# Gate weights loaded first, two weight splits moved into the attention, late rows transposed one group later

## The chip, the cores and the metric

One core of one Trainium2 chip runs the whole program. The metric is the device time of one execution in microseconds (us), the median over several runs. The engines are TensorE (PE, its weight loads PEld), VectorE (DVE), ScalarE (ACT), GpSimd (POOL) and SyncE (SP), which here only issues transfers.

## What is computed

The reference chains three stages over 4 batches of 576 tokens.

```python
# attention: 4 x 8 heads, 576 positions, 64 columns a head
scores = q @ k.T / sqrt(64) + min(-(cum_i - cum_j), 0)     # cum = cumsum(max(s, 0)); causal
x = softmax(scores) @ v                                    # -> x: 2304 tokens x 512
# one expert of 8 for each token, the one with the largest logit
logits = x @ w_gate                                        # w_gate: 512 x 8
x[t] = p_e * (relu(x[t] @ w1[e]) @ w2[e])                  # 512 -> 1024 -> 512
# gated unit on normalised rows
xn = x / rms(x) * rms_g
out = (silu(xn @ w_gate2) * (xn @ w_val)) @ w_out          # 512 -> 1536 -> 512
```

## The kernel before

**The attention** (`attention`, L573) works on 16 pairs of heads, `p` = 0 to 15. For each pair TensorE makes scores (`s_mm`, L269 to L284), VectorE adds the bias and takes the row extreme (L255), ScalarE takes exponentials (`s_exp`, L295), TensorE transposes the probabilities in seven groups (`t_mm`, L314), ScalarE copies them out of PSUM (L347), TensorE multiplies by `v` (`pv_mm`, L360 and L364), ScalarE copies the result (L370, L372), and TensorE turns it back to token rows (`o_mm`, L388). That last product has as its moving operand the tile `tg`: 128 columns of the identity, which turn the rows, and 16 columns of `w_gate`, which give the gate's logits in the same instruction.

The order of the work is written by hand. `attention` fills a list `plan` with (time, function) entries; a pair's step stands at 10 `p` plus an offset from the table `POS`, and single steps have times of their own. The entries are sorted by time and called in that order. What they emit for TensorE, VectorE, ScalarE and SP stays in that order on each engine; GpSimd's order is chosen by the scheduler. The times are only ranks: one unit of the plan is a little over a microsecond on the chip. Ahead of the plan stand the loads of pairs 0 and 1 (query, key, bias, and last `load_v` for both).

**The gate weights.** `gate_consts` (L122), planned at 14.0, makes `tg`: GpSimd clears the gate columns (L125), VectorE copies the identity (L126), SP issues two transfers of `w_gate` (L128), each 64 partitions x 4 x 8 numbers, told to come after the cumulated sums are stored. Planned just ahead of them, at 12.6 to 12.8, are three fills (`prefill`, L155) of 771 KB each, which preset rows of the scratch tensor `xs`.

**The weights of an expert** come as eight raw pieces of 512 KB in two halves for each of four units. `feed` (L647) issues the transfer of the next piece into one of four staging buffers, `split` (L658) makes a piece into a rounded part, by a cast on ScalarE (L666), and a remainder, by a subtraction on GpSimd (L667), and then may call `feed` once more. For the first expert, `feed` runs for two pieces at 60.0 and `split` at the six times of `PIECES` (L568), of which the first four fetch another piece. The unit that the last two pieces fill lies in a slot that held inputs of the attention's last pair.

**Routing and early rows.** When a batch is done, `route` (L412) finds each token's expert and its place (VectorE, L434 to L477), and GpSimd scatters the rows into `xs`, a region for each expert, by indirect transfers (L482). The last batch's steps are spread over the first expert by the counts in `RANK` (L977): so many steps behind each group. The first 256 rows of the first expert ("early") are loaded once the third batch is scattered: `EARLY_AT` has the load (152.2, L691), the scaling by the gate's probability (164.0, `gate`, L736) and the transposes (170.2, 170.3).

**The first expert** (`moe`, L877) fetches its last two pieces, runs eight groups of the first product (`gemm1`, L783), with a split behind groups 0 and 1, then four groups of the second (`gemm2`, L803). Its next 128 rows ("late") need the last batch's scatter: `load_late` (L705) is issued in the middle of `gemm1`, then the second expert's rows and its first four pieces. Behind group 0 of `gemm2` stands the scaling of the late rows, behind group 1 their transposes (`turn_tile`, L761), the first split of the second expert's weights behind those, then groups 2 and 3 and the row-wise product of the late rows (`rows_gemm1`, L835, L841). `moe` is emitted as a list of its own behind the attention's; in the trace its first two fetches stand earlier on SP's queue, between the attention's loads.

```python
    feed(k, 2)                                  # moe: the first expert's last two pieces
    for f in range(8):
        gemm1(k, 0, f, NA)
        ...
        if f < 2:
            split(k, 1, False)
    ...
    gemm2(k, 0, 0, NA)
    gate(k, k.xl, ((0, 128),))
    gemm2(k, 0, 1, NA)
    turn_tile(k, k.xl[:, 0, :], *xb)
    split(k)
    gemm2(k, 0, 2, NA)
```

Of the kernel before, what the change touches and what calls it, by code (L numbers as in the profile page):

```python
# [15 lines left out]
B, H, S, D = 4, 8, 576, 64  # L16
# [6 lines left out]
NA = 256  # L23
# [98 lines left out]
def gate_consts(k):  # L122
    nc = k.nc
    k.tg = k.apool.tile([128, H // 2, 144], F32, name="tg")
    nc.gpsimd.memset(k.tg[:, :, 128:144], 0.0)  # L125
    nc.vector.tensor_copy(k.tg[:, :, 0:128], k.ident.unsqueeze(1).broadcast_to((128, H // 2, 128)))  # L126
    for h, r in enumerate((slice(0, 64), slice(64, 128))):
        i = nc.sync.dma_start(out=k.tg[r, :, 128 + 8 * h:136 + 8 * h],  # L128
                              in_=k.w_gate.rearrange("d (a b) e -> d a b e", b=2)[:, :, h, :])
        after(k, i.ins, [k.cumdone])  # L130


def cumulate(k):
# [81 lines left out]
def attn_load(k, p):  # L215
    nc = k.nc
    st = k.st[p] = Ctx()
    st.q, st.k, st.cb, st.cm, st.bd = k.inp[p % 3]
    st.s = {}
    nc.sync.dma_start(out=st.q, in_=k.q[p])  # L220
    nc.sync.dma_start(out=st.k, in_=k.k[p])
# [179 lines left out]
def after(k, ins, earlier):  # L401
    for x in earlier:
        k.tc.add_manual_dep(ins, x.name, SYNC, reason="rows of one tensor")
# [161 lines left out]
)  # L565
ROUTE = (34.1, 0.2)
FR = 2
PIECES = (80.0, 81.5, 90.0, 91.5, 159.0, 166.0)  # L568
EARLY_AT = (152.2, 164.0, 170.2, 170.3)
FILL = (12.6, 12.7, 12.8, 22.6, 22.7, 22.8, 32.5, 32.6)  # L570

# [1 line left out]
def attention(k):  # L573
    k.st, k.todo = {}, []
    with ExitStack() as es:
        k.apool = es.enter_context(k.tc.tile_pool(name="attn", bufs=1))
        cum = cumulate(k)
        next(cum)
        masks(k)
        attn_statics(k)  # L580
        next(cum)
        attn_load(k, 1)
        for _ in cum:
            pass
        load_bias(k, 1)
        load_v(k, 0)
        load_v(k, 1)
        plan = []

        def add(at, fn, *a):  # L590
            plan.append((at, len(plan), fn, a))

        def step(j):
            next(j, None)

        k.order = [(0, u, q) for u in range(4) for q in (0, 2)]
        k.staged, k.xq, k.who = [], {}, {}

        for p in range(NP):
            for tag, fn in (("S", s_mm), ("X", s_exp), ("T", t_mm), ("V", pv_mm), ("W", pv_out), ("O", o_mm)):  # L600
                for i, at in enumerate(POS[tag]):
                    add(10 * p + at, fn, k, p, i)
            add(10 * p + POS["N"][0], s_norm, k, p)
            for h, at in enumerate(POS["Q"]):
                add(max(10 * p + at, 0.5), q_diag, k, p, h)
            for fn, at in zip((attn_load, load_bias, load_v), POS["Z"]):
                if p > 1:
                    add(10 * p + at, fn, k, p)
            j = route(k, p // 4)
            if p == NP - 1:  # L610
                k.last = j
            elif p % 4 == 3:
                for n in range(RSTEPS):
                    add(10 * p + ROUTE[0] + ROUTE[1] * n, step, j)
        add(60.0, feed, k, FR)
        for n, at in enumerate(PIECES):
            add(at, split, k, 1, n + FR < len(PIECES))
        add(EARLY_AT[0], load_early, k)
        add(EARLY_AT[1], lambda k: gate(k, k.x[0], EARLY), k)
        add(EARLY_AT[2], lambda k: x_transpose(k, 0, (0, 1), EARLY), k)  # L620
        add(EARLY_AT[3], lambda k: x_transpose(k, 0, (2, 3), EARLY), k)
        add(13.0, rank_consts, k)
        add(14.0, gate_consts, k)
        for n in range(FILLS):
            add(FILL[n], prefill, k, n)
        for at, n, fn, a in sorted(plan, key=lambda x: x[:2]):
            fn(*a)
# [19 lines left out]
def feed(k, n=1):  # L647
    for _ in range(n):
        if k.order:
            s, u, q = k.order.pop(0)  # L650
            raw = staging(k, [2, 512], F32)
            src = (k.w1, k.w2)[u // 2]
            src = src[0, u % 2] if s == 0 else src[bass.ds(who(k, s), 1), u % 2].rearrange("e p q n -> (e p) q n")
            k.nc.sync.dma_start(out=raw, in_=src[:, q:q + 2, :])
            k.staged.append((s, u, q, raw))


def split(k, n=1, refill=True):  # L658
    nc = k.nc
    for _ in range(n):  # L660
        if k.staged:
            s, u, q, raw = k.staged.pop(0)
            if q == 0:
                new_unit(k, s, u)
            w = k.wt[s, u][:, q:q + 2]
            nc.scalar.copy(w[:, :, 0, :], raw)  # L666
            nc.gpsimd.tensor_tensor(w[:, :, 1, :], raw, w[:, :, 0, :].bitcast(F32), op=ALU.subtract)  # L667
            if refill:
                feed(k)
# [66 lines left out]
def gate(k, x, tiles):  # L736
    for t, m in tiles:
        k.nc.scalar.activation(x[0:m, t, 0:DM], x[0:m, t, 0:DM], AF.Copy, scale=x[0:m, t, DM + 1:DM + 2])
# [138 lines left out]
def moe(k, close):  # L877
    k.y, k.sq = {}, {}

    def rank(n):  # L880
        for _ in range(n):
            next(k.last, None)

    feed(k, 2)
    k.order = [(s, u, q) for s in range(1, E) for u in range(4) for q in (0, 2)]
    row = ids(k, k.x[0], EARLY)
    keep_ids(k, row, 0)
    rank(RANK[0])
    for f in range(8):
        gemm1(k, 0, f, NA)  # L890
        rank(RANK[f + 1])
        if f == 3:
            load_late(k)
        if f < 2:
            split(k, 1, False)
    load_x(k, 1)
    feed(k, STG)
    first = tiles_of(CAP[0])
    gemm2(k, 0, 0, NA)
    rank(1)  # L900
    gate(k, k.xl, ((0, 128),))
    gemm2(k, 0, 1, NA)
    rank(1)
    xb = [k.rpool.tile([128, 4, CM], F32R, name=f"xb{n}", tag=f"xt{n}", bufs=1)[:, :, 0:128] for n in range(2)]
    turn_tile(k, k.xl[:, 0, :], *xb)
    row = ids(k, k.xl, ((0, 128),))
    keep_ids(k, row, column(k, 1))
    split(k)
    gemm2(k, 0, 2, NA)
    gate(k, k.x[1], first)  # L910
    split(k)
    gemm2(k, 0, 3, NA)
    split(k)
    k.hr = y_tile(k, "hr")[:, 0:1024]
    rows_gemm1(k, xb, 0)
    split(k)
    rows_gemm1(k, xb, 1)
    hb = [k.mpool.tile([128, 8, CM], F32R, name=f"hb{n}", tag=f"h{n}")[:, :, 0:128] for n in range(2)]
    turn_tile(k, k.hr[:, 0:512], *[t[:, 0:4] for t in hb])
    x_transpose(k, 1, (0, 1), first)  # L920
    turn_tile(k, k.hr[:, 512:1024], *[t[:, 4:8] for t in hb])
    x_transpose(k, 1, (2, 3), first)
    split(k)
    y = finish(k, 0, NA)
    row = ids(k, k.x[1], first)
    yr = k.hr.rearrange("p (a n) -> p a n", a=2)
    k.yr = yr[:, 0, :]
    rows_gemm2(k, hb)
    keep(k, y, NA, 0)
    keep_ids(k, row, column(k, 2))  # L930
    split(k)
    head = iter(())
    for s in range(1, E):
        last = s == E - 1
        n = CAP[s - 1]
        if last:
            close()
            glu_first(k)
            next(head)
        else:  # L940
            load_x(k, s + 1)
        for f in range(8):
            gemm1(k, s, f, n)
            if s == 1 and f == 0:
                y = yr[:, 1, :].rearrange("p (c n) -> p c n", c=4)
                turn_rows(k, k.yr, y)
            if s > 1 and f == 1:
                y = finish(k, s - 1, CAP[s - 2])
            if f == 5:
                keep(k, y, CAP[s - 2] if s > 1 else LATE, column(k, s))  # L950
                if not last:
                    gate(k, k.x[s + 1], tiles_of(CAP[s]))
            if f % 2 or (s == 1 and f < 4):
                split(k)
            next(head, None)
        for c in range(4):
            gemm2(k, s, c, n)
            if not last:
                if c in (1, 2):
                    x_transpose(k, s + 1, (2 * c - 2, 2 * c - 1), tiles_of(CAP[s]))  # L960
                if c == 1:
                    row = ids(k, k.x[s + 1], tiles_of(CAP[s]))
                if c == 3:
                    keep_ids(k, row, column(k, s + 2))
            split(k)
            if s == E - 2 and c == 0:
                head = glu_head(k)
            next(head, None)
    assert not k.staged and not k.order

    def tail():
        keep(k, finish(k, E - 1, CAP[-1]), CAP[-1], column(k, E))

    k.tail = tail
# [764 lines left out]
```

## Time and profile before

| | us |
|---|---|
| median of 3 runs | 881.94 (880.71 to 884.03) |
| the profiled execution | 880.62 |
| its span, first to last instruction | 878.6 |
| granted TensorE clock, mean over the span | 0.987 |
| TensorE busy | 844.7 |

The trace is of one execution, whose own time is 880.62 us; the span is what its instructions cover. Rows of a timeline have the start in us, the duration in us, the engine, the line of the kernel, the operation, the output and its inputs by the program's names, and a count where neighbours are merged; a bracket has the time for which the engine was idle before it and what released it. A count xN with one duration is the stretch from the first start to the last end.

### The profile page before, as it was taken

The numbers are of one execution on the slowest core, as the hardware profiler recorded it, in microseconds if no ns is written. First come the engines' busy times: TensorE is split into PE (matmuls) and PEld (weight loads), VectorE is DVE, ScalarE is ACT, GpSimd is POOL, SyncE is SP. The second block draws the span as 40 slices with busy tenths as digits, with TensorE's granted clock in tenths as the row PEclk, the third lists the DMA queues.
The fourth block names the chain that finished last, engine by engine and source line by source line (L and its number), as shares of the span: only waits on it lengthen the run. The fifth ranks groups of instructions, "written<-read, shape, count | busy, mean of one in ns | idle before, by whom it ended". The sixth has DMA issues, their size and how long they took to land.

```text
span 878.6 us, 15491 instructions
## 1 busy us (share of the span) xinstructions
PE 844.7 (96%) x5522; PEld 754.1 (86%) x5522; DVE 513.7 (58%) x1241; ACT 455.4 (52%) x1069; POOL 366.4 (42%) x318
## 2 busy tenths in 40 slices
PE   6699999999899999999999999999999999999994
PEld 4477777769799999999999999999999988888883
DVE  5356666657433355335799998988898878400000
ACT  4688998883665565566553443333333244433310
POOL 3000422034476666767331332544444360466641
PEclk9899999999899999999999999999999999999997
DMA  6997887221765565557562433332222487520001
GB/s 210 291 308 237 263 254 214 82 79 56 222 198 185 183 206 191 171 192 208 184 220 100 141 109 102 114 106 92 102 103 101 138 323 316 194 95 37 36 37 40
DMA packets 60506, 141.45 MB, mean 161 GB/s; under 512 B 6992, under 2 KB 25451, under 8 KB 60419
## 3 DMA queue, kind: packets, MB, share of 16 engines
q1 hardware_dynamic: 57459, 130.83, 46.1%
q0 software_dynamic: 2912, 9.46, 2.9%
q8 instruction: 45, 0.74, 0.4%
q14 instruction: 42, 0.34, 0.1%
q10 hardware_dynamic: 48, 0.07, 0.0%
HBM read 105.42 MB, written 34.92 MB: 160 GB/s over the span
## 4 chain that ended last, share of the span: by engine, by line
PE 47%; DVE 3%; ACT 1%; issue 0%; POOL 0%; POOLq 0%; DVEq 0%; ACTq 0%
PE gg L1165 29%; PE go L1481 17%; PE g L803 1%; DVE raw L1094 0%; DVE ws L1142 0%; DVE gx1a L1409 0%; DVE raw L1097 0%; DVE h L787 0%; DVE raw L1093 0%; DVE sq L828 0%; DVE tmp L1187 0%; DVE tmp L1185 0%; ACT raw L1095 0%; ACT ws L1137 0%; DVE y L831 0%
## 5 line engine op out<-in xcount | busy, mean ns | idle before, releaser
L667 POOL TENSOR_TENSOR u<-raw,u 128x1024 fp32r<-128x1024 f32 x64 | 154.9, 2434 | 84.0 <-ACT u L666 83.8
L803 PE MATMUL g<-h,u 128*128 128x256 f32 (+7 forms) x768 | 107.8, 299 | 0.6 <-DVE h L787 0.3
L803 PEld LDWEIGHTS g<-h,u 128*128 128x128 f32 x768 | 103.4, 192 | 1.7 <-DVE h L787 0.8
L783 PE MATMUL g<-xt,u 128*128 128x256 f32 (+7 forms) x768 | 104.3, 295 | 0.0
L783 PEld LDWEIGHTS g<-xt,u 128*128 128x128 f32 x768 | 101.4, 188 | 0.8
L255 DVE CUSTOM_DVE_ANT_0 sc<-s,in 128x128 f32<-128x128 f32 (+3 forms) x128 | 57.8, 489 | 32.7 <-ACT vp L372 19.2
L295 ACT ACTIVATE p<-sc,nm 128x128 f32<-128x128 f32 (+3 forms) x128 | 71.0, 574 | 7.2 <-DVE nm L255 7.2
L1203 POOL TENSOR_TENSOR hs<-tmp,hs 128x384 f32<-128x384 f32 x27 | 30.3, 1123 | 106.0 <-ACT hs L1201 106.0
L666 ACT CAST u<-raw 128x1024 fp32r<-128x1024 f32 x64 | 67.1, 1049 | 4.2 <-DMA raw<-in_w 4.2
L1165 PE MATMUL gg<-gx2a,ws 128*128 128x384 f32 x360 | 67.4, 335 | 0.6 <-DVE tmp L1187 0.6
L1165 PE MATMUL gg<-gx0a,ws 128*128 128x384 f32 x360 | 67.7, 336 | 0.0
L1165 PE MATMUL gg<-gx1a,ws 128*128 128x384 f32 x360 | 67.1, 335 | 0.0
L1486 DVE COPY raw<-go 128x256 f32<-128x256 f32 x1 | 0.4, 425 | 109.3 <-ACT raw L1485 109.3
L811 DVE TENSOR_TENSOR sq<-sq,sn 128x256 f32<-128x256 f32 (+6 forms) x21 | 14.4, 688 | 84.1 <-ACT sn L810 84.1
L1165 PEld LDWEIGHTS gg<-gx2a,ws 128*128 128x128 f32 x360 | 62.7, 188 | 0.9 <-DVE tmp L1187 0.9
L1165 PEld LDWEIGHTS gg<-gx0a,ws 128*128 128x128 f32 x360 | 63.1, 188 | 0.0
L1165 PEld LDWEIGHTS gg<-gx1a,ws 128*128 128x128 f32 x360 | 62.7, 188 | 0.0
L347 ACT COPY pt<-t 128x512 f32<-128x512 f32 (+3 forms) x160 | 56.0, 448 | 10.3 <-PE t L314 9.1
L314 PE MATMUL t<-ident,p 128*128 128x128 f32 x400 | 51.8, 275 | 0.0
L1095 ACT ACTIVATE raw<-raw 128x512 f32<-128x512 f32 x36 | 24.5, 682 | 51.1 <-DVE raw L1094 32.9
L269 PE MATMUL s<-in 64*128 64x128 f32 (+3 forms) x256 | 49.5, 495 | 0.0
L360 PE MATMUL pvy<-pt,vp 128*64 128x512 f32 (+4 forms) x320 | 46.9, 428 | 1.1 <-ACT pt L347 1.1
(307 smaller groups left out, 1714.6 us busy)
## 6 DMA issues: line engine op xcount, KB each, us to landing
raw<-in_w SPq DMA_DIRECT2D x64, 512.0 KB, 4.7
hd<-hs SPq DMA_DIRECT2D x72, 192.0 KB, 1.9
in<-cumd SPq DMA_DIRECT2D x30, 256.0 KB
xs<-zrow SPq DMA_DIRECT2D x8, 771.0 KB, 10.6
raw<-in_wg SPq DMA_DIRECT2D x12, 512.0 KB, 4.1
raw<-in_wv SPq DMA_DIRECT2D x12, 512.0 KB
raw<-in_wo SPq DMA_DIRECT2D x12, 512.0 KB, 7.6
vp<-in_v SPq DMA_DIRECT2D x16, 320.0 KB, 5.2
```

Source lines behind the costliest of these rows:

```text
L255: k.nc.vector.tensor_tensor_reduce(out=out, in0=ps, in1=bias, scale=-0.125, scalar=3e38, op0=ALU.add, op1=ALU.min, accum_out=accum)
L269: nc.tensor.matmul(ps[h], st.q[r, 128 * i:128 * i + 128], st.k[r, 0:w], start=True, stop=False)
L295: k.nc.scalar.activation(out, st.s[i, h][:, 0:w], AF.Exp, bias=st.nm[:, n:n + 1], scale=-1.0, accum_out=acc)
L314: nc.tensor.transpose(ps[:, off:off + 128], src[:, 128 * j:128 * j + 128], k.ident)
L347: nc.scalar.copy(b, a)
L360: nc.tensor.matmul(st.y[r, a - 64:512], st.v[:, h, j, :], k.pt[:, h, o:o + S - a], start=j == 0, stop=j == 4)
L666: nc.scalar.copy(w[:, :, 0, :], raw)
L667: nc.gpsimd.tensor_tensor(w[:, :, 1, :], raw, w[:, :, 0, :].bitcast(F32), op=ALU.subtract)
L783: nc.tensor.matmul(ps[:, 0:n], w[:, f % 4, a, 128 * kc:128 * kc + 128], x[b][:, kc, 0:n], start=kc == 0 and i == 0, stop=kc == 3 and i == 2)
L803: nc.tensor.matmul(ps[:, 0:n], w[:, f % 4, a, 128 * c:128 * c + 128], k.h[b][:, f, 0:n], start=f == 0 and i == 0, stop=f == 7 and i == 2)
L1165: k.nc.tensor.matmul(k.ps[u, bank], w[:, a, 128 * c:128 * c + 128], x[:, b, GT * c:GT * c + GT], start=first and c == 0 and n == 0, stop=c ...
L1481: k.nc.tensor.matmul(acc[g][t], c[:, a, cols], w[:, b, :], start=f == 0 and i == 0, stop=f == NF - 1 and i == 2)
```

## The change

Three edits. `gate_consts` is planned at 0.7 instead of 14.0, without VectorE's copy of the identity, which becomes `gate_ident` and stays at 14.0. `PIECES` has eight times instead of six, and the number that decides whether a split fetches another piece follows its length, so that six of them do; the two fetches and the two splits in the first expert go. In the first expert the scaling of the late rows moves behind group 1 of the second product, and group 2 is put ahead of their transposes.

```diff
@@ gate_consts
     nc.gpsimd.memset(k.tg[:, :, 128:144], 0.0)
-    nc.vector.tensor_copy(k.tg[:, :, 0:128], k.ident.unsqueeze(1).broadcast_to((128, H // 2, 128)))
     for h, r in enumerate((slice(0, 64), slice(64, 128))):
...
+def gate_ident(k):
+    k.nc.vector.tensor_copy(k.tg[:, :, 0:128], k.ident.unsqueeze(1).broadcast_to((128, H // 2, 128)))
@@
-PIECES = (80.0, 81.5, 90.0, 91.5, 159.0, 166.0)
+PIECES = (80.0, 81.5, 90.0, 91.5, 159.0, 161.7, 164.4, 167.1)
@@ attention
-        add(14.0, gate_consts, k)
+        add(0.7, gate_consts, k)
+        add(14.0, gate_ident, k)
@@ moe
-    feed(k, 2)
...
-        if f < 2:
-            split(k, 1, False)
...
     gemm2(k, 0, 0, NA)
     rank(1)
-    gate(k, k.xl, ((0, 128),))
     gemm2(k, 0, 1, NA)
     rank(1)
+    gate(k, k.xl, ((0, 128),))
+    gemm2(k, 0, 2, NA)
...
     turn_tile(k, k.xl[:, 0, :], *xb)
     row = ids(k, k.xl, ((0, 128),))
     keep_ids(k, row, column(k, 1))
     split(k)
-    gemm2(k, 0, 2, NA)
     gate(k, k.x[1], first)
     split(k)
     gemm2(k, 0, 3, NA)
```

## Rows read from the trace of the kernel before

**Rows 1.** The page, part 1: busy us, share of the span, instructions.

```profile
PE 844.7 (96%) x5522; PEld 754.1 (86%) x5522; DVE 513.7 (58%) x1241; ACT 455.4 (52%) x1069; POOL 366.4 (42%) x318
```

**Rows 2.** Timeline of TensorE: the wait for `tg`, and the same step later.

```profile
39.49 1.30 PE L388 MATMUL tl<-tg,vp 128*128 128x144 f32 x4 [6.87 <-DMA tg<-in_w_gate]
...
43.33 1.14 PE L360 MATMUL pvy<-pt,vp 128*64 128x512 f32 x4
...
162.10 0.93 PE L314 MATMUL t<-ident,p 128*128 128x128 f32 x7
...
164.78 1.08 PE L360 MATMUL pvy<-pt,vp 128*64 128x512 f32 x4
```

**Rows 3.** Timeline of SP's queue, 12 to 36 us: issues of transfers.

```profile
14.85 0.43 SPq L220 DMA_DIRECT2D in<-in_q  x1
...
15.80 1.31 SPq L228 DMA_DIRECT2D in<-cumd  x2
...
29.67 2.69 SPq L128 DMA_DIRECT2D tg<-in_w_gate  x2
```

**Rows 4.** Timeline of VectorE: the first use of pair 2's bias.

```profile
27.43 0.29 DVE L255 CUSTOM_DVE_ANT_0 sc<-s,in 128x128 f32<-128x128 f32 x1 [1.43 <-DMA in<-cumd]
```

**Rows 5.** Timeline of ScalarE at the end of the attention.

```profile
190.91 2.36 ACT L347 COPY pt<-t 128x512 f32<-128x512 f32 x5
193.09 1.42 ACT L738 ACTIVATE x<-x 128x512 f32<-128x512 f32 x2
194.32 1.22 ACT L347 COPY pt<-t 128x256 f32<-128x256 f32 x5
```

**Rows 6.** Timeline of TensorE: the last pair's value product.

```profile
195.09 1.08 PE L360 MATMUL pvy<-pt,vp 128*64 128x512 f32 x4 [1.06 <-ACT pt L347]
```

**Rows 7.** SP's queue (a raw piece, the early rows), and the page's row of raw pieces.

```profile
118.24 0.34 SPq L654 DMA_DIRECT2D raw<-in_w  x1
...
188.51 0.38 SPq L691 DMA_DIRECT2D x<-xs  x1
...
raw<-in_w SPq DMA_DIRECT2D x64, 512.0 KB, 4.7
```

**Rows 8.** Timelines of VectorE (routing, two batches) and of GpSimd (subtractions of two splits).

```profile
177.32 0.19 DVE L459 TENSOR_TENSOR ob<-oh,base 128x40 f32<-128x40 bf16 x1
...
177.76 0.16 DVE L465 TENSOR_SCALAR xt<-tid 128x5 f32<-128x5 f32 x1
...
205.08 1.88 DVE L459 TENSOR_TENSOR ob<-oh,base 128x40 f32<-128x40 bf16 x1
...
207.21 2.08 DVE L465 TENSOR_SCALAR xt<-tid 128x5 f32<-128x5 f32 x1
...
204.50 4.75 POOL L667 TENSOR_TENSOR u<-raw,u 128x1024 fp32r<-128x1024 f32 x2 [5.58 <-ACT u L666]
```

**Rows 9.** Timeline of TensorE: the first expert's second product and what follows.

```profile
212.46 5.81 PE L803 MATMUL g<-h,u 128*128 128x256 f32 x48
222.58 1.11 PE L765 MATMUL xq<-ident,xl 128*128 128x128 f32 x4 [4.31 <-ACT xl L738]
...
223.56 7.81 PE L803 MATMUL g<-h,u 128*128 128x256 f32 x48
231.21 5.74 PE L841 MATMUL r<-u,xb 128*128 128x512 f32 x24
```

**Rows 10.** Timeline of ScalarE: the late rows' scaling, the second expert's first cast.

```profile
221.81 0.72 ACT L738 ACTIVATE xl<-xl 128x512 f32<-128x512 f32 x1 [5.66 <-DMA xl<-xs]
...
227.73 1.05 ACT L666 CAST u<-raw 128x1024 fp32r<-128x1024 f32 x1 [3.21 <-DMA raw<-in_w]
```

**Rows 11.** SP's queue: the second expert's first four pieces.

```profile
221.63 2.08 SPq L654 DMA_DIRECT2D raw<-in_w  x4
```

**Rows 12.** Windows of 1 us: busy PE, PEld, DVE, ACT, POOL; PEclk; DMA share; GB/s.

```profile
195.00:196.00 1.00, 0.91 (x4) 0.34 (x6) 0.00 (x0) 1.00 (x5) 0.00 (x0) 1.00 0.00 0
...
221.00:222.00 1.00, 0.00 (x0) 0.00 (x0) 0.00 (x0) 0.20 (x1) 0.00 (x0) 0.50 0.82 103
```

## The prediction

> **What bounds the kernel now.** I read the page's busy line first: TensorE is busy for 96% of the span [rows 1], so a change pays only where it closes a hole in TensorE's row or opens one. I then read TensorE's own waits, and after them its timeline around each. Between the first matmul and the end of the first expert three holes matter. The first is early: the first gate-and-transpose matmuls (`tl`) stand still for 6.87 us until the transfer of `w_gate` into `tg` has landed, and what follows is slow [rows 2]. The second is small: at the end of the attention the last pair's value product waits 1.06 us for ScalarE's copies of the transposed probabilities [rows 6]. The third is in the first expert: the transposes of the late rows wait 4.31 us for their scaling [rows 9]. Everything between is TensorE work end to end; what I predict is what becomes of these three holes. All times below are on the clock of the profiled execution of before, unless I say "shifted".
>
> **Part 1, gate weights at the head.** The two `w_gate` transfers are issued at 29.67, behind three fills of `xs`, and take 2.69 us of SP's queue [rows 3]. The new place is right behind the first two loads of `v`, ahead of the query load issued at 14.85 [rows 3]. Their only other condition, the cumulated sums, is met by then, since bias loads that need the same sums were issued earlier. So `tg` starts 14.8 us earlier and is needed no sooner than 32.62 (39.49 less 6.87): the wait goes. What is late next there? In a later, undisturbed pair the step from the end of the transposes (162.10 + 0.93 = 163.03) to the value product takes 1.75 us, to 164.78 [rows 2]. Before, the same step ran from 32.62 to 43.33, 10.71 us [rows 2]. The gain is 10.71 - 1.75 = **9.0 us**: 6.87 of wait, the rest matmuls that ran slowly after it.
> The price: the two issues, at the 2.69 us they took, now stand ahead of pair 2's query, key and bias loads on SP. VectorE's first use of pair 2's bias is at 27.43, and its wait before that is put down to a bias transfer [rows 4]; that transfer was issued from 15.80 on [rows 3]. If it truly landed only then, TensorE could lose up to 2.69 us later through ScalarE; if it landed earlier, nothing. I take nothing, since a matmul feeds the same instruction and ended just before, and keep 2.7 for the range. VectorE's copy of the identity into `tg` keeps its place and its length.
>
> **Part 2, the last two splits in the attention.** Each split is a cast on ScalarE, 1.05 us [rows 10], and a subtraction on GpSimd, 4.75 us for two [rows 8]. Nothing is added in number; what counts is where they now stand. In the plan, the split at 161.7 comes after the first of the last pair's seven probability copies, the one at 164.4 after the fifth and after the scaling of the early rows, the one at 167.1 behind all of them. Before, only one split stood near, behind them all. ScalarE works without a pause from the first of these copies (190.91) through the scaling (193.09) to the last copies (194.32) [rows 5], and TensorE's value product at 195.09 is already waiting for it [rows 6]. Two casts in between delay it by 2 x 1.05, less a little overlap: **2.0 us lost**, a hole of 3.1 us in place of 1.06. No cover is left for them: the copies are the next thing that TensorE wants.
> There is a second price. Two raw weight pieces were fetched early, the first issued at 118.24 [rows 7]. In the new plan their fetches follow the splits at 159.0 and 161.7, so on SP's queue they stand behind the load of the early rows, which SP issues only at 188.51, when the scatters have finished [rows 7]. The first is then issued at about 189.0. The page's median from issue to landing for these pieces is 4.7 us [rows 7]; behind a row load the first of four, issued at 221.63, was there for the cast at 227.73, 6.1 us later [rows 10, 11]. It lands between 193.7 and 195.1. ScalarE reaches its cast at 193.09 + 1.42 + 1.0 = 195.4 (rows 5, and the first added cast): no wait, with 0.3 us to spare at the worse end.
> What it frees: in the first expert the two subtractions held VectorE. The first step of routing took 1.88 us at 205.08 where it takes 0.19 elsewhere, another 2.08 at 207.21 against 0.16, and both ended with a GpSimd subtraction (204.50 + 4.75 = 209.25) [rows 8]. Without them the routing chain, the scatters behind it and the load of the late rows come **3.6 us** earlier, which is worth nothing until part 3.
>
> **Part 3, late rows one group on.** Before, from the start of the second product's first two groups (212.46) to the row-wise product (231.21) there are 18.75 us [rows 9]. With the transposes behind group 2 the work is four groups (2 x 5.81, the time of two at full clock [rows 9]) and the transposes at full clock, half of the 0.98 between 222.58 and 223.56 [rows 9]: 12.1 us. The gain is **6.6 us**, if the rows are ready. They were scaled at 221.81 + 0.72 = 222.5 [rows 10]; the attention's loss adds 2.0 and the freed VectorE takes off 3.6, so 220.9. They are wanted after three groups: 212.46 + 2.0 + 1.5 x 5.81 = 223.2. That is 2.3 us in hand.
> What is late next: the second expert's rows and weights are issued behind the late rows on SP, so they too come 1.6 us earlier, the first raw piece at 226.1 instead of 227.73 [rows 10]. The row-wise products take 5.74 us [rows 9], from 226.6 to 232.3, then transposes follow that need ScalarE. From 226.1 ScalarE has four casts of 1.05, three row tiles at 0.71 each (1.42 for two [rows 5]) and a few short copies, which ends at about 232 to 233.5. I take nothing, and 1.0 for the range.
>
> **The sum:** -9.0 + 2.0 - 6.6 = -13.6 us. The profiled execution took 880.62 (a span of 878.6 and 2.0 around it), so 867.0; the median of the runs, 881.94, is 1.3 above it, so **868.3**. One per two hundred, 4.4 us, is about what a measurement of this kernel can tell from no change.
>
> **The rivals.**
> *The clock falls in the new hole.* TensorE's granted clock was still full (1.00, 2.4 GHz) in the stretch after the idle 1.06 us, and half (0.50, 1.2 GHz) at the end of the idle 4.31 [rows 12]; the new hole of 3.1 us lies between. After the 4.31, 48 matmuls took 7.81 us instead of 5.81 and the transposes 0.98 instead of half [rows 9]: 2.5 us. If the same is lost in the value product, 870.8. The Trainium skill says this too (TensorE: Matmul & The Clock Gate, Part 1: The HAM clock gate): the throttled clock is the idle default and activity releases it. By that rule a wait put in front of TensorE costs more than its length, which speaks against part 2; the trace agrees, with 0.50 before the late rows. I give it 0.25.
> *An input of the saturated opening takes the gate weights' place.* 2.7 us of part 1 go: 871.0. For it, the named bias transfer [rows 4]; against it, TensorE had no other wait there. 0.10.
> *VectorE is not freed,* say because its slow steps had another cause. The late rows are then scaled at 224.5, 1.3 us after they are wanted: 869.6. Against it, the steps end with the subtraction. 0.05.
> *Slower: the fetched piece stops ScalarE.* The cast at 164.4 waits in order in front of the copies that the value product needs, so each microsecond by which its raw piece lands after 195.4 is one on TensorE. It eats the whole gain from a landing at 209.0 on, 20 us after its issue; no such piece shows more than 6.1 [rows 10, 11]. Above that it is slower than before. For that 0.02; for a landing one to four us late, the sum at 869 to 875, another 0.06.
> *The change doesn't do what it says:* `tg` still lands late, because it queues behind something at the head too. Only parts 2 and 3 are left, 4.6 us: 877.3. 0.02.
>
> **How the numbers follow.** The forecast has 0.50. The range reaches down to 866.0 (the two casts hidden after all, 866.3, and the runs' spread) and up to 873.5 (clock and bias together, 868.3 + 2.5 + 2.7), which leaves out the late landings and the two last rivals. Faster by over 0.5% needs less than 877.5: all but the slower rival, the change that doesn't do what it says and a part of the late landings: 0.94. Within 0.5%: 0.04. Slower: 0.02.
>
> **What would show it.** Part 1: no wait of `tl` for `tg`; pair 1's value product at about 34.4 instead of 43.33 and every later piece of the attention 9 us earlier; the clock at 1.00 through 35 to 45. Part 2: four casts among the last pair's copies, TensorE's wait there near 3.1 us, on ScalarE; the two routing steps at 0.2 us each. Part 3: no wait of the late transposes, 12.1 us between the two products, the row-wise one starting at about 217.6 (226.6 shifted by 9.0). It would be wrong if a wait on a bias or query transfer showed before 60 us, if the cast at 164.4 waited for its transfer, or if the second expert's weights opened a new hole after the row-wise products.

## The result, and the profile after

The changed kernel took 869.25 us in the median of four runs (866.87 to 870.34), the kernel before 882.14 in four runs beside them (880.71 to 884.03). The ratio is 0.9849, with an interval from 0.982 to 0.9878. The median fell by 12.9 us, to 869.25 where 868.3 was forecast. The profiled execution, the fastest of the four, took 866.87, with a span of 865.1; the forecast sum for one execution, -13.6, stands against 865.1 - 878.6 = -13.5.

In the rows below, the line numbers of the changed kernel are 3 or 4 higher than before; only the transfers of the gate weights, L128, are now L127. TensorE's waits first, to the middle of the span (time in all, times, longest); the rows left out are of 0.4 us or less:

```profile
PE cb L149 <- POOL p L245: 7.8, 1, 7.8
PE pvy L363 <- ACT pt L350: 2.9, 1, 2.9
...
```

The first row is the wait for the cumulated sums ahead of the first matmul; it is as long as before. The two large waits, for `tg` [rows 2] and for the late rows [rows 9], are gone. The small one has grown from 1.06 [rows 6] to 2.94 us. TensorE's timeline at pair 0's value product and at the three places:

```profile
23.82 1.08 PE L363 MATMUL pvy<-pt,vp 128*64 128x512 f32 x4
...
32.40 0.66 PE L391 MATMUL tl<-tg,vp 128*128 128x144 f32 x4
...
34.31 1.08 PE L363 MATMUL pvy<-pt,vp 128*64 128x512 f32 x4
...
187.89 1.08 PE L363 MATMUL pvy<-pt,vp 128*64 128x512 f32 x4 [2.94 <-ACT pt L350]
...
188.91 1.90 PE L363 MATMUL pvy<-pt,vp 128*64 128x448 f32 x16
...
205.24 8.64 PE L807 MATMUL g<-h,u 128*128 128x256 f32 x72
213.72 0.60 PE L769 MATMUL xq<-ident,xl 128*128 128x128 f32 x4
...
217.09 5.74 PE L845 MATMUL r<-u,xb 128*128 128x512 f32 x24
...
232.07 1.88 PE L787 MATMUL g<-xt,u 128*128 128x312 f32 x12
```

Read it as a running difference to before. At pair 0's value product the two traces are still together (23.82, and 23.87 before). Pair 1's value product starts at 34.31 instead of 43.33, 9.02 earlier [rows 2]. The last pair's starts at 187.89 instead of 195.09 [rows 6], only 7.20 earlier: nearly all of what has been given back is the growth of the wait, 2.94 - 1.06 = 1.88. The row-wise product starts at 217.09 instead of 231.21 [rows 9], 14.1 earlier. The span ends 13.5 earlier; the 0.6 between is lost much later, where the gated unit's waits on VectorE are 1.4 us in all instead of 0.8.

SP's queue has `tg` where the plan put it, and the raw pieces that were feared to be late:

```profile
14.85 1.26 SPq L127 DMA_DIRECT2D tg<-in_w_gate  x2
...
179.42 0.38 SPq L695 DMA_DIRECT2D x<-xs  x1
179.90 0.89 SPq L658 DMA_DIRECT2D raw<-in_w  x2
```

ScalarE's timeline at the end of the attention, and in the first expert:

```profile
181.82 0.62 ACT L350 COPY pt<-t 128x512 f32<-128x512 f32 x1
182.30 1.09 ACT L670 CAST u<-raw 128x1024 fp32r<-128x1024 f32 x1
183.25 1.88 ACT L350 COPY pt<-t 128x512 f32<-128x512 f32 x4
184.94 1.42 ACT L742 ACTIVATE x<-x 128x512 f32<-128x512 f32 x2
186.18 1.11 ACT L670 CAST u<-raw 128x1024 fp32r<-128x1024 f32 x1
187.11 1.23 ACT L350 COPY pt<-t 128x256 f32<-128x256 f32 x5
188.11 1.17 ACT L670 CAST u<-raw 128x1024 fp32r<-128x1024 f32 x1
...
211.63 0.73 ACT L742 ACTIVATE xl<-xl 128x512 f32<-128x512 f32 x1
```

Two casts stand between the copies that the value product needs. None of these rows has a bracket: ScalarE never stood still, so the whole 2.94 us of TensorE's wait is ScalarE's own work. The late rows were scaled by 212.36, 1.36 us before their transposes began. VectorE's two routing steps, 1.88 and 2.08 us before [rows 8]:

```profile
197.41 0.19 DVE L462 TENSOR_TENSOR ob<-oh,base 128x40 f32<-128x40 bf16 x1
...
197.84 0.16 DVE L468 TENSOR_SCALAR xt<-tid 128x5 f32<-128x5 f32 x1
```

Windows of the changed kernel (columns as in [rows 12]): the clock stayed at 1.00 in the opening and in the idle of 2.94.

```profile
35.00:40.00 5.00, 5.00 (x54) 2.90 (x50) 2.98 (x16) 4.57 (x17) 0.00 (x0) 1.00 1.05 271
...
186.00:187.00 1.00, 0.00 (x0) 0.00 (x0) 0.00 (x0) 1.00 (x2) 0.00 (x0) 1.00 0.01 4
...
188.00:189.00 1.00, 1.00 (x10) 0.43 (x12) 0.00 (x0) 1.00 (x4) 1.00 (x1) 1.00 0.00 0
```

### The profile page after: what moved, and what is told of

Read it like the earlier page. It is cut to its first block, busy times and chain, and to the rows that moved or that the text cites. A ratio compares the mean times of both kernels' runs of the same rounds, so it can differ in the third digit from the quotient of the medians.

```text
span 865.1 us, 15488 instructions
## 1 busy us (share of the span) xinstructions
PE 840.1 (97%) x5522; PEld 750.3 (87%) x5522; DVE 507.6 (59%) x1241; ACT 454.4 (53%) x1069; POOL 365.9 (42%) x318
## 4 chain that ended last, share of the span: by engine, by line
PE 47%; DVE 3%; DMA 1%; ACT 1%; issue 1%; POOL 0%; POOLq 0%; DVEq 0%; ACTq 0%
PE gg L1166 28%; PE go L1482 17%; PE g L807 1%; DMA ringa<-ytd 1%; DVE raw L1095 0%; DVE ws L1143 0%; DVE gx1a L1410 0%; DVE raw L1098 0%; DVE h L791 0%; DVE ringa L1062 0%; DVE raw L1125 0%; DVE raw L1094 0%; DVE sq L832 0%; DVE tmp L1188 0%; DVE tmp L1186 0%
## 5 line engine op out<-in xcount | busy, mean ns | idle before, releaser
L807 PE MATMUL g<-h,u 128*128 128x256 f32 (+7 forms) x768 | 105.9, 295 | 0.7 <-DVE h L791 0.4
L807 PEld LDWEIGHTS g<-h,u 128*128 128x128 f32 x768 | 101.4, 188 | 1.8 <-DVE h L791 0.9
```

Source lines behind the costliest of these rows:

```text
L807: nc.tensor.matmul(ps[:, 0:n], w[:, f % 4, a, 128 * c:128 * c + 128], k.h[b][:, f, 0:n], start=f == 0 and i == 0, stop=f == 7 and i == 2)
```

## The experiments

The runs fell on four chips, called A to D here. The kernel before ran on each beside them and took 880.5, 890.8, 892.56 and 882.42 us in the median, so times are compared on one chip or as ratios. Each diff is against the changed kernel.

**Part 1 alone (chip A).** Parts 2 and 3 undone.

```diff
-PIECES = (80.0, 81.5, 90.0, 91.5, 159.0, 161.7, 164.4, 167.1)
+PIECES = (80.0, 81.5, 90.0, 91.5, 159.0, 166.0)
...
+    feed(k, 2)
...
+        if f < 2:
+            split(k, 1, False)
...
     rank(1)
+    gate(k, k.xl, ((0, 128),))
     gemm2(k, 0, 1, NA)
     rank(1)
-    gate(k, k.xl, ((0, 128),))
-    gemm2(k, 0, 2, NA)
...
     split(k)
+    gemm2(k, 0, 2, NA)
```

> Only part 1: the gate weights' transfers at the head, the splits and the late rows as before. My theory (each hole has its own price): the wait for tg and the slow matmuls after it go, 9.0 us, so about 871.6 us at a span of 869.6 and a ratio near 0.990; the hole of 1.06 us at the last pair's value product and the one of 4.31 us before the late rows' transposes stay as they were. Rival (the early loads of pair 2, now behind the gate weights, take some of it back): a new wait before 60 us, up to 2.7 us, so up to 874.3.

Measured: 871.18 (870.32 to 875.1), ratio 0.9886 (0.9869 to 0.9902), which is 9.3 us less than 880.5. Both other holes are still there, in TensorE's timeline (of the slowest of the five executions):

```profile
185.10 1.08 PE L363 MATMUL pvy<-pt,vp 128*64 128x512 f32 x4 [1.06 <-ACT pt L350]
...
212.38 1.12 PE L769 MATMUL xq<-ident,xl 128*128 128x128 f32 x4 [4.11 <-ACT xl L742]
...
213.36 8.14 PE L807 MATMUL g<-h,u 128*128 128x256 f32 x48
```

So part 1 is worth its forecast 9.0 within the spread, and no input of the opening took the gate weights' place. The 48 matmuls behind the third hole took 8.14 here and 7.81 before, against 5.81 without a hole [rows 9]. This execution, at 875.1, lost time elsewhere too: at 423 us the granted clock fell to 0.50 for some 6 us, behind waits of 0.78 us and less.

**Parts 1 and 3, without part 2 (chip A, again on chip C).**

```diff
-PIECES = (80.0, 81.5, 90.0, 91.5, 159.0, 161.7, 164.4, 167.1)
+PIECES = (80.0, 81.5, 90.0, 91.5, 159.0, 166.0)
...
+    feed(k, 2)
...
+        if f < 2:
+            split(k, 1, False)
```

> Parts 1 and 3 without part 2: the last two fetches and splits are back in the first expert, the late rows still one group later. My theory: the value product's wait falls back from 2.9 to about 1.1 us, which gives 1.9 us; the two routing steps take about 1.9 and 2.1 us again, the late rows are scaled at about 213.5 and wanted at about 211.9, a hole of 1.6 us; the second expert's weights come 1.9 us later than in the changed kernel and open a further hole of 1 to 2 us before the turned hidden rows. Together 0.7 to 1.7 us slower than the changed kernel, 869.5 to 871 us. Rival (part 2 is a pure loss, the late rows are in time anyway): 1.9 us faster than the changed kernel, about 867.

Measured on A: 868.01 (865.9 to 870.72), ratio 0.985 (0.9832 to 0.9868). Its timeline of TensorE, where three holes of 1.0 to 1.7 us stand in place of one of 2.94:

```profile
23.28 1.08 PE L363 MATMUL pvy<-pt,vp 128*64 128x512 f32 x4 [0.26 <-ACT pt L350]
...
185.47 1.08 PE L363 MATMUL pvy<-pt,vp 128*64 128x512 f32 x4 [1.04 <-ACT pt L350]
...
213.11 0.66 PE L769 MATMUL xq<-ident,xl 128*128 128x128 f32 x4 [1.66 <-ACT xl L742]
...
223.52 0.66 PE L769 MATMUL xq<-ident,hr 128*128 128x128 f32 x4 [1.25 <-ACT hr L847]
...
232.89 1.88 PE L787 MATMUL g<-xt,u 128*128 128x312 f32 x12
```

The routing steps take as long as before, and the second ends with GpSimd's subtractions (194.86 + 4.75 = 199.61); VectorE's and GpSimd's timelines:

```profile
195.44 1.88 DVE L462 TENSOR_TENSOR ob<-oh,base 128x40 f32<-128x40 bf16 x1
...
197.56 2.08 DVE L468 TENSOR_SCALAR xt<-tid 128x5 f32<-128x5 f32 x1
```

```profile
194.86 4.75 POOL L671 TENSOR_TENSOR u<-raw,u 128x1024 fp32r<-128x1024 f32 x2 [5.55 <-ACT u L670]
```

The second expert starts at 232.89, against 232.07 in the changed kernel. But this execution was already 0.54 ahead at pair 0's value product (23.28, against 23.82), before anything that part 2 changes. From there to the second expert it took 209.61 us, against 208.25: in the traces part 2 nets 1.4 us, as was expected, but less than the spread of the runs.

> Parts 1 and 3 without part 2, now beside the changed kernel. The trace of its first run, set against that of the changed kernel, says: 1.9 us gained at the value product, 1.7 us lost before the late rows' transposes and 1.25 us before the turned hidden rows, so 1 to 1.4 us slower than the changed kernel where the clock holds behind the 2.9 us hole, and 0.5 us faster to equal where it falls. Rival (part 2 is worth several us by freeing VectorE): more than 2.5 us slower.

Measured on C: 877.6 (873.58 to 882.28), ratio 0.9843 (0.9815 to 0.987); the changed kernel beside it had the same ratio, 0.9843 (below). Part 2 as it was made gains nothing that the medians can tell. That is what was expected for executions in which the clock falls in the changed kernel's hole, and on C it did (below).

**Parts 1 and 2, the late rows where they were (chip A).**

```diff
     rank(1)
+    gate(k, k.xl, ((0, 128),))
     gemm2(k, 0, 1, NA)
     rank(1)
-    gate(k, k.xl, ((0, 128),))
-    gemm2(k, 0, 2, NA)
...
     split(k)
+    gemm2(k, 0, 2, NA)
```

> Parts 1 and 2 without part 3: scaling and transposes of the late rows one group earlier, as before. Theory A (part 2 alone frees the third hole): the late rows land at about 209.7 and are scaled by 210.4, the transposes are wanted at 211.05, so no hole, and the time is that of the changed kernel within 0.5 us. Theory B (part 3 is what removes the hole): a hole of 2 us or more before the late rows' transposes and a lower clock after it, 2 to 4.5 us slower than the changed kernel, 871 to 873.5 us.

Measured: 867.16 (866.33 to 868.95), ratio 0.9846 (0.9829 to 0.9862). ScalarE's timeline and TensorE's:

```profile
210.56 0.72 ACT L742 ACTIVATE xl<-xl 128x512 f32<-128x512 f32 x1 [1.64 <-DMA xl<-xs]
```

```profile
211.33 0.66 PE L769 MATMUL xq<-ident,xl 128*128 128x128 f32 x4 [0.29 <-ACT xl L742]
...
217.58 5.75 PE L845 MATMUL r<-u,xb 128*128 128x512 f32 x24
```

With the routing freed, the late rows are nearly in time even one group earlier. The row-wise product starts at 217.58, against 217.09: in the trace part 3 is worth 0.5 us on top of part 2. Parts 2 and 3 are two cures of the same hole.

**The gate weights behind the other opening loads, ahead of the fills (chip A, one run).**

```diff
-        add(0.7, gate_consts, k)
+        add(12.55, gate_consts, k)
```

> The changed kernel with the gate weights' transfers planned at 12.55 instead of 0.7: behind the loads of pairs 2 and 3, but ahead of the three fills of the scratch rows. Theory A (the fills of 771 KB were what held the gate weights): issue near 24 us, landing before 32.4 us, no wait of tl for tg, the time of the changed kernel within 0.5 us. Theory B (the whole saturated queue holds them): a wait of 1 to 6 us at tl remains.

Measured: 867.26, span 865.3. SP's queue and TensorE's timeline:

```profile
25.03 1.25 SPq L127 DMA_DIRECT2D tg<-in_w_gate  x2
```

```profile
31.65 0.66 PE L391 MATMUL tl<-tg,vp 128*128 128x144 f32 x4
...
187.15 1.26 PE L363 MATMUL pvy<-pt,vp 128*64 128x512 f32 x4 [2.94 <-ACT pt L350]
...
188.40 3.35 PE L363 MATMUL pvy<-pt,vp 128*64 128x448 f32 x16
...
206.18 8.64 PE L807 MATMUL g<-h,u 128*128 128x256 f32 x72
```

No wait of `tl`: what made `tg` late was to stand behind the three fills, not to stand behind the opening's other loads. Issued at 25.03 it is still in time, so the place at the very head was not needed. (Two single transfers, `gv` and `tokd`, issued between the loads and the fills, were passed as well; they were not tried apart.) The run also shows what the rival on the clock foresaw, behind a hole of the same 2.94 us (windows):

```profile
188.00:189.00 1.00, 1.00 (x8) 0.45 (x6) 0.00 (x0) 0.75 (x2) 1.00 (x2) 0.50 0.00 0
```

From this value product to the second product it took 206.18 - 187.15 = 19.03 us, in the changed kernel 205.24 - 187.89 = 17.35: the lower level cost 1.7 us.

**The changed kernel on chip B**, no edit, beside the next three.

> The changed kernel once more, beside the runs below on the same chip. 867 to 870 us, the hole before the last pair's value product 2.9 us. Theory A (a hole of this length sometimes lets the granted clock fall and sometimes not): its runs are spread over some 2 us, and its profile shows either a clock of 1.00 through the hole and the value product in 2.9 us, or 0.50 behind the hole and the way from the value product to the second product longer by 1.5 to 2.5 us. Theory B (the clock is not touched by a hole of 2.9 us): always 1.00.

Measured: 876.24 (874.91 to 876.8), ratio 0.9839 (0.9815 to 0.9862). The hole was 4.21 us and the clock fell behind it (TensorE's timeline):

```profile
193.95 1.97 PE L363 MATMUL pvy<-pt,vp 128*64 128x512 f32 x4 [4.21 <-ACT pt L350]
...
195.93 3.63 PE L363 MATMUL pvy<-pt,vp 128*64 128x448 f32 x16
```

The two rows of `pvy` took (1.97 - 1.08) + (3.63 - 1.90) = 2.6 us more than in the first trace of the changed kernel; up to the second product it was 20.17 instead of 17.35 us.

**The casts out of the chain of copies (chips B, C, D).** All eight splits stay in the attention; the two at 159.0 and 161.7 go to 150.0 and 151.5, and the one at 164.4 goes behind the last copies.

```diff
-PIECES = (80.0, 81.5, 90.0, 91.5, 159.0, 161.7, 164.4, 167.1)
+PIECES = (80.0, 81.5, 90.0, 91.5, 150.0, 151.5, 165.3, 167.1)
```

> The changed kernel with the last four splits at 150.0, 151.5, 165.3 and 167.1: two a pair earlier, two behind all the copies of transposed probabilities, so that none stands ahead of the copies that the last value product waits for; the two fetches then also stand ahead of the early rows' load. My theory (the cost of part 2 is the casts' place on ScalarE): the value product's wait falls from 2.9 to under 0.5 us, the rest stays, 2.4 to 2.9 us faster than the changed kernel, 865 us or less. Rival (another work, the value copies or GpSimd, takes the casts' place as the bound): the wait stays over 1.5 us, or a new wait of 1 us or more opens a pair earlier; no gain over 1 us.

Measured on B: 872.01 (870.1 to 873.2), ratio 0.9787 (0.9762 to 0.9813), 4.2 us less than the changed kernel there. Its last value product, in TensorE's timeline, and a wait earlier that is taken up in the last section:

```profile
181.29 0.71 PE L317 MATMUL t<-ident,p 128*128 128x128 f32 x3 [2.03 <-ACT pt L350]
...
193.05 1.08 PE L363 MATMUL pvy<-pt,vp 128*64 128x512 f32 x4 [0.74 <-ACT pt L350]
```

> The kernel with the four casts out of the chain once more, to see what it gains on a chip where the hole is 2.9 us. My theory: the hole falls to under 0.5 us and no lower clock follows, 2.4 us faster than the changed kernel where the clock held and up to 4.2 us where it fell. Rival (its gain of 4.2 us on the other chip came from that chip's standstill of ScalarE alone): under 1 us faster.

Measured on C: 873.49 (871.64 to 880.72), ratio 0.9811 (0.9779 to 0.9844), with a wait of 1.37 us ahead of the last value product, not under 0.5. The changed kernel beside it, no edit:

> The changed kernel once more, beside the two runs below. On a chip where ScalarE does not stand still before the last pair: a hole of 2.9 us before the last value product, 867 to 870 us at a before of 880 to 883; where it does, a hole of 4.2 us with the clock at half behind it, 874 to 877 at a before of 888 to 892.

Measured on C: 878.16 (875.17 to 880.22), ratio 0.9843 (0.9817 to 0.9869), with a hole of 2.77 us ahead of the last value product and the products behind it at 1.97 instead of 1.08. The two ratios' intervals overlap; the medians stand 4.7 us apart, in the direction of chip B.

> The kernel with the four casts out of the chain a third time, in the hope of a chip on which ScalarE does not stand still before the last pair. If it does not: the wait of the last value product under 0.5 us, the clock at 1.00 throughout, a ratio to the kernel before of about 0.982 (13.6 + 2.4 us of 881). If it does: a wait of 0.7 to 1.4 us as in the two earlier runs and a ratio of 0.979 to 0.981. Rival (without the standstill the casts gain nothing over the changed kernel): a ratio of 0.985.

Measured on D: 864.26 (863.99 to 867.45), ratio 0.9798 (0.9776 to 0.9821). ScalarE's timeline, and TensorE's:

```profile
182.75 1.33 ACT L742 ACTIVATE x<-x 128x512 f32<-128x512 f32 x2
183.98 1.13 ACT L350 COPY pt<-t 128x256 f32<-128x256 f32 x5
184.97 2.04 ACT L670 CAST u<-raw 128x1024 fp32r<-128x1024 f32 x2
```

```profile
22.78 1.08 PE L363 MATMUL pvy<-pt,vp 128*64 128x512 f32 x4 [0.26 <-ACT pt L350]
...
184.67 1.08 PE L363 MATMUL pvy<-pt,vp 128*64 128x512 f32 x4 [0.75 <-ACT pt L350]
```

The value product starts at 184.67, against 187.89 in the first trace of the changed kernel. Of that 3.22, 1.04 is there from pair 0 on (22.78, against 23.82) and doesn't come from the edit. The other 2.2 is the fall of the wait from 2.94 to 0.75, about the two casts of 1.05 that no longer stand between the copies. What is left, 0.75, was expected below 0.5; the scaling of the early rows (1.33) still stands between the copies, as it did before, where the wait was 1.06. This version is faster than both kernels. The changed kernel did not run on chip D, so there the step from it rests on the ratios (0.9798 against 0.9839 to 0.9849).

**One more cast ahead of the last copies (chip B).**

```diff
-PIECES = (80.0, 81.5, 90.0, 91.5, 159.0, 161.7, 164.4, 167.1)
+PIECES = (80.0, 81.5, 90.0, 91.5, 159.0, 161.7, 164.4, 164.5)
```

> The changed kernel with the last split at 164.5 instead of 167.1: a third cast ahead of the copies that the last value product waits for. My theory: the wait grows by one cast's 0.95 us to 3.9 us, one for one on TensorE, plus up to 1.2 us if its raw piece lands late; the hole is then long enough that the granted clock is at half speed behind it, which costs 1.5 to 2.5 us more: 2.5 to 4.5 us slower than the changed kernel. Rival 1 (the clock holds): 0.95 us slower. Rival 2 (TensorE has slack behind the hole): no change.

Measured: 877.03 (876.22 to 880.12), ratio 0.9858 (0.9831 to 0.9884), and in TensorE's timeline:

```profile
195.64 1.97 PE L363 MATMUL pvy<-pt,vp 128*64 128x512 f32 x4 [5.17 <-ACT pt L350]
```

The hole grew by 5.17 - 4.21 = 0.96: a cast in this place goes into TensorE's wait one for one. The median grew by 0.8, which the spread of the runs doesn't tell from nothing. The further loss by the clock did not come, because on this chip the clock had already fallen behind the hole of the changed kernel.

**Parts 2 and 3, without part 1 (chip B, one run).**

```diff
-        add(0.7, gate_consts, k)
+        add(14.0, gate_consts, k)
```

> Parts 2 and 3 without part 1: the gate weights at 14.0 as before. My theory (the parts add up): the wait of 6.9 us for tg is back with slow matmuls after it, the other holes are those of the changed kernel, 9.0 us slower than it, about 877 us. Rival (part of the 9.0 us would be given back later in any case): less than 7 us slower.

Measured: 886.25, 10.0 more than the changed kernel's median on that chip; the absolute time was expected for a chip like A. TensorE's timeline has the old wait, a little longer:

```profile
40.36 1.30 PE L391 MATMUL tl<-tg,vp 128*128 128x144 f32 x4 [7.73 <-DMA tg<-in_w_gate]
```

Part 1's share is about the same with and without the other two, as far as one run tells.

## Why the prediction was right

**Part 1** came as worked out, 9.02 in the trace and 9.3 by itself. The cost of its issues was mis-sized: 2.69 us had been carried over from [rows 3], where the same two issues stood behind the fills; at the head they took 1.26. It changed nothing, since the cost was taken as hidden. The rival on the opening's inputs is refuted: no wait on a bias or query transfer shows in TensorE's list.

**Part 2, the casts.** The hole was forecast at 3.1 and is 2.94; the loss of 2.0 is 1.88. "No cover is left for them" was the step that carried it, and the runs bear it out from both sides: taking the casts out lowers the hole to 0.75, one more raises it by 0.96. The raw piece that might have stopped ScalarE was in time, and its cast at 186.18 shows no wait.

**Part 2, the routing.** The two steps fell to 0.19 and 0.16. Reckoned from the last value product, the late rows were there 4.04 earlier than before (221.81 - 195.09 = 26.72, against 210.56 - 187.88 = 22.68 in the run of parts 1 and 2), where 3.6 was forecast. The Trainium skill (SBUF — State Buffer, Who interferes with whom) has the mechanism: a VectorE instruction with two operands in SBUF and a GpSimd instruction that reads SBUF exclude each other for a whole instruction. The trace agrees for the step with two operands, 1.88 beside a subtraction and 0.19 without one. The second step has one tensor operand and went the same way, 2.08 and 0.16; why is not shown.

**Part 3.** 205.24 to 217.09 is 11.85 us, forecast 12.1. What the working passed over is that its 6.6 is not part 3's own. It said that the freed routing "is worth nothing until part 3"; the runs show that either part alone removes most of the third hole, 0.29 being left with part 2 and 1.66 with part 3. The sum was right because the two were costed together. That it agrees to 0.1 is luck: at the row-wise product the trace had gained 14.1, not 13.6, since part 3's stretch came out shorter and part 2's loss smaller than forecast, and 0.6 of that went again in the gated unit, which the working doesn't touch.

**The clock.** In the profiled execution the clock held through the 2.94, so the likeliest case came. The rival came too, in other executions: 1.7 us on chip A with the gate weights just ahead of the fills, 2.6 for the changed kernel on chip B, against 2.5 in the forecast. Over the four runs of the result the time goes with the mean granted clock: 866.87 at 0.995, 868.42 at 0.993, 870.07 at 0.992, 870.34 at 0.991. That would fit both cases taking turns in one kernel. But the clock also fell far from the three holes: in the traces of part 1 alone and of parts 1 and 3, at 423 and 420 us, behind waits of 0.78 us and less. Only the first of the four has a trace, so where the others lost their clock is not shown.

## What to carry to other kernels

When two edits shorten the same wait, cost each one alone as well as both: here part 2, with its price on ScalarE, added 1.4 us to what part 3 had already bought where the clock held, and nothing that the medians show. Work moved onto an engine in front of a copy that TensorE is about to want goes into TensorE's wait one for one; with the same casts about ten units of the plan earlier, or just behind the copies, the wait was 2.2 us shorter in the traces without a standstill, and the medians 4.2 and 4.7 us lower on the two chips where both kernels ran. A transfer that lands late is best read with what stands ahead of it on its queue: here, being just ahead of three fills was enough.

## What the runs showed that was not expected

**The same idle time, two clocks.** Behind an idle 2.94 us the granted clock was 1.00 (2.4 GHz) in two executions (the changed kernel, and parts 1 and 2) and 0.50 (1.2 GHz) in a third (the gate weights ahead of the fills); on chip C it was 0.50 behind an idle 2.77. The Trainium skill calls the throttled clock the idle default, which activity releases (TensorE: Matmul & The Clock Gate, Part 1: The HAM clock gate). The falls agree; the two executions that held show that an idle time of this length need not lead there, so a hole of this kind has a price with two values.

**A standstill of ScalarE on two chips.** On chips B and C, ScalarE stood idle in the last pair but one, while GpSimd issued its five scatters (173.09 to 179.07 on B). ScalarE's timeline of the changed kernel on B:

```profile
178.11 0.58 ACT L350 COPY pt<-t 128x512 f32<-128x512 f32 x1 [2.82 <-PE tl L391]
...
180.26 2.12 ACT L350 COPY pt<-t 128x512 f32<-128x512 f32 x5 [1.57 <-PE tl L391]
```

In the first trace, on chip A and on chip D this idle time is absent. The version without casts in the chain stood idle in the same pair on B, which is its wait of 2.03 above; the changed kernel has a wait of 2.07 there on C. The two batches before show the like: set against the first trace, the value products of the changed kernel fall back by 0.5, 2.1 and 2.2 us on B and by 1.8, 2.7 and 4.2 on C, each time at the five scatters of a batch, and by at most 0.3 in between. On B these 4.8 us, the longer hole (1.3) and the way at the lower clock behind it (2.8) are nearly all of the 9.1 us by which the span is longer than in the first trace. Whether this also makes the hole of the changed kernel 4.21 on B is not shown (on C it was 2.77). Its cause was not found, and no run was made for it; the comparisons rest on the kernel before, which ran beside on the same chip.
